# The first inverse's store on ScalarE's queue, a corner's copies ahead of a weight piece, and a chunk's keys behind three pieces

## The chip, the cores and the metric

One Trainium2 chip, one core of it. The metric is device time in microseconds (us), the median of several runs. The trace comes from one further execution under the hardware profiler; its times are counted from the start of its span. PE is TensorE, DVE VectorE, ACT ScalarE, POOL GpSimd, and SP is SyncE, which here only issues transfers.

## The reference: a delta-rule recurrence, then a multiplicative feed-forward

```python
# q, k, v: (4, 8, 768, 48) = batch, heads, steps, head size; beta: (4, 8, 768)
k_n = k / (np.linalg.norm(k, axis=-1, keepdims=True) + 1e-06)
for t in range(S):
    y[:, :, t] = np.einsum('bhd,bhde->bhe', q[:, :, t], state)
    v_old = np.einsum('bhde,bhd->bhe', state, kt)
    state = state + bt[:, :, :, None] * np.einsum('bhd,bhe->bhde', kt, vt - v_old)
x = y.transpose(0, 2, 1, 3).reshape(3072, 384)
out = ((x @ w1) * (x @ w2)) @ w3 @ w_out      # w1, w2: 384x1024; w3: 1024x1024; w_out: 1024x384
```

All of it is float32.

## The kernel before

**Chunks.** The 768 steps are cut into 12 chunks of 64. Inside a chunk the recurrence is a triangular solve. For each chunk `m`, `scores` (L357) multiplies keys by keys and by queries, and leaves `U` (L379, the scaled strictly triangular part) and `PT` (the masked products of keys and queries). The inverse of the unit triangular matrix is made in two steps. The diagonal 32x32 blocks of two chunks at a time are rearranged through DRAM: `to_blocks` stores them to `Ud` (L414, four transfers a chunk), `inverse(j)` loads them as `Ub` (L426), runs 31 elimination steps on DVE (L440 and L445), and stores the result to `Vd` (L453). For pairs 0 and 1 the elimination works in a PSUM bank, and ACT copies the result back to `Vb` (L449). Then `corner(m)` reads the blocks back: four transfers `TT<-Vd` (L462) and four `T22<-Vd` (L469). It makes the off-diagonal 32x32 corner with one DVE transpose (L481), two sets of products on PE (L498), and two ACT copies after each set (L514 and L525; the second writes the corner into `TT`).

**The chain over chunks.** `chain(c)` multiplies state and keys (L551, `S,KQ`), subtracts from the values (DVE, `R`, L584), multiplies by the inverse (L551, `R,TT`), scales (`X`, L594), multiplies by the keys and adds to the state (`S`, L613 or L615). `outputs(c)` makes y on PE (L652); ACT copies it to `xT` (L673), and transfers move some of its rows within SBUF (L684), six each for chunks 0 and 1.

**The feed-forward.** `w3 @ w_out` is folded into one matrix first (`transpose_w3`, L750 and L753, and `fold`, L759 and L766). Then `ab` multiplies `xT` by `w1` and `w2` (L779), ACT and DVE multiply the two (L791, L795), and later products with the folded matrix follow (L874). Weights come in 36 pieces: `piece` loads one into one of five `raw` buffers (L699), and ACT (L707, L708), DVE (L710, L711) and POOL (L715) rewrite it; after POOL's step the buffer is free. Pieces P24 to P29 are `w1`, P30 to P35 `w2`. `w2s` is at first the room of `w_out`, so P30 and its like also wait for folds.

**Queries and keys.** `load_perm(m)` loads a chunk's keys and then its queries in a permuted order, eight transfers each (L230: `kperm`, `qperm`), and DVE transposes them (L324). `p4.0` below is the keys of chunk 4, the fifth chunk.

**The order.** The order on every engine is fixed by hand. The text `ORDER` names generators: each word runs one more step of that part, and `in_text_order` (L159) ties the instructions of each engine to that order. So a word that stands later than another issues its instructions behind the other's on each engine that both use; on an engine that they don't share, nothing is ordered between them. Each engine, SP's queue too, works its line off in order and stands still at an instruction whose inputs or buffers are not ready. Steps that matter here, counted from 0:

- `P30.0` issues a piece's loads on SP, `P30.1` its ACT part, `.2` DVE, `.3` POOL.
- `V0.36` is the second of ACT's copies L449, `V0.37` the store of `Vd`; `V1.1` the load of `Ub`.
- `e0.0` is corner 0's eight copies on SP, `e0.1` DVE's L481, `e0.5` ACT's L525.
- `u2`, `u3` are the stores to `Ud`; `p4.0` the keys of chunk 4; `c1.0` to `c1.3` are chunk 1's `S,KQ`, `R`, `R,TT` and `X`.

SP issues every transfer, but for those of chunk 0's keys and queries at the start, which ACT issues.

Of the kernel before, what the change touches and what calls it, by code (L numbers as in the profile page):

```python
# [44 lines left out]
V0 P4 V0 P19 P19 P19 P6 f0 P16 P17 P17 V0 V0 P16 V0 V0 P17 P7 f2 k3 P14 p2 V0 V0 v1 P19 P15 f1  # L45
f0 g1 f1 t11 V0 d2 t11 P15 f2 f5 V0 P14 P15 f0 P16 v0 P17 V0 V0 V0 V0 g1 P20 f5 V0 f2 f5 t6 t9
P15 t6 P20 t7 V0 n1 P22 P20 V0 t7 d2 s0 V0 V0 f3 P23 P20 P22 t8 P21 V0 n0 P24 n0 f3 V0 V0 n1 t8
V0 V0 t9 V0 V0 s2 p3 f4 f3 P23 P22 P26 g1 V0 g1 V0 f4 g1 P21 P22 P23 t14 d3 f4 P23 g1 t12 p3 V0
N1 P30 t12 t14 t15 e0 t15 d3 f7 d3 f6 e0 P30 P21 e0 e0 P24 f7 s2 s2 e1 e0 s2 P24 e0 e1 V1 p4 s2
e1 P26 s2 e1 P25 d3 c0 P21 P30 u2 s3 c0 s3 P26 N1 P31 P24 y0 s3 s3 y0 c0 s3 s3 P25 t13 N1 e1 u3  # L50
P31 c0 P26 P31 P32 c1 V1 c1 e1 P25 V1 P27 c1 V1 c1 V1 V1 t13 V1 V1 V1 V1 V1 V1 y0 V1 P25 f7 f6
f6 P30 P32 P32 v2 V1 P27 s1 P31 V1 V1 y1 b3 b1 V1 b0 P32 P28 y1 b1 V1 b1 b3 P29 P27 b2 b3 y1 V1
P27 b1 b0 P29 P29 c1 a01 b2 a03 P28 V1 a01 a00 b3 P28 P29 a02 a02 a03 P35 P28 V1 a05 b7 a00 V1
V1 V1 V1 a06 P33 V1 b5 a05 b7 b0 V1 P34 V1 b5 V1 a06 V1 V1 V1 P34 k4 V1 P35 V1 g2 a00 V1 k5 a00
# [35 lines left out]
def kernel(  # L90
# [36 lines left out]
    def half(z):  # L127
        return slice(C * z, C * z + C)

    def feat(z):  # L130
        return slice(C * z, C * z + D)
# [6 lines left out]
    def in_turn(pool, shape, tag, n, name, dt=FP32):  # L138

        i = turns.get(tag, -1)  # L140
        while True:
            i = turns[tag] = (i + 1) % n
            if (tag, i) not in held:
                return pool.tile(shape, dt, tag=f"{tag}{i}", name=name, bufs=1)

    def two_banks():
        return in_turn(psW, [P, 2, 512], "w", 2, "ps_w")
# [11 lines left out]
    def in_text_order():  # L159
# [7 lines left out]
    pe, dve, act, pool, sync = nc.tensor, nc.vector, nc.scalar, nc.gpsimd, nc.sync  # L167
# [7 lines left out]
        out=strict[:], in_=strict[:], pattern=[[1, P]], compare_op=ALU.is_gt,  # L175
# [7 lines left out]
    def padded(name, shape, n, start=0):  # L183
        res = []
        for i in range(n):
            t = persist.tile(shape, FP32, name=f"{name}{i}")
            pool.memset(t[:, start:] if start else t[:], 0.0)
            res.append(t)
        return res

    TTs = padded("TT", [P, NR, H, C], 2)
# [3 lines left out]
    ktoks, vtoks, KQs, PTs, Xs, Ss = {}, {}, {}, {}, {}, {}  # L195
# [114 lines left out]
    def scale_of(x, m, crossed=0):  # L310
        j, cc = divmod(m, 2)
        return x[j][:, cc] if x is ns else x[j][:, crossed, cc]
# [92 lines left out]
    Uds, Vds = {}, {}  # L405
# [14 lines left out]
    def inverse(j):  # L420
        Vb = in_turn(work, [P, BS, BS], "Vb", 1, "Vb")
        pool.memset(Vb[:], 0.0)
        pool.memset(Vb[:].rearrange("p s t -> p (s t)")[:, 0 : BS * BS : BS + 1], 1.0)
        yield
        U = in_turn(work, [P, BS, BS], "Ub", 1, "Ub")
        sync.dma_start(out=U[:], in_=Uds.pop(j)[:])  # L426
        yield
        V = Vb
        if j < 2:

            V = two_banks().rearrange("p a (s t) -> p (a s) t", t=BS)
            held.add(("w", turns["w"]))
            for i in range(0, BS, BS // 2):
                act.copy(out=V[:, i : i + BS // 2], in_=Vb[:, i : i + BS // 2])
                yield
        for s in range(BS - 1):
            n = BS - 1 - s
            t = in_turn(work, [P, 256], "tb", 2, "tb")
            tv = t[:, 0 : (s + 1) * n].rearrange("p (r t) -> p r t", t=n)
            dve.tensor_tensor(  # L440
                out=tv, in0=V[:, 0 : s + 1, s : s + 1].to_broadcast([P, s + 1, n]),
                in1=U[:, s, s + 1 : BS].unsqueeze(1).to_broadcast([P, s + 1, n]), op=ALU.mult,
            )
            o = V[:, 0 : s + 1, s + 1 : BS]
            dve.tensor_tensor(out=o, in0=o, in1=tv, op=ALU.subtract)  # L445
            yield
        if j < 2:
            for i in range(0, BS, BS // 2):
                act.copy(out=Vb[:, i : i + BS // 2], in_=V[:, i : i + BS // 2])  # L449
                yield  # L450
            held.clear()
        Vds[j] = in_turn(dram, [P, BS, BS], "Vd", 2, "Vd")
        sync.dma_start(out=Vds[j][:], in_=Vb[:])  # L453
        yield

    T11s = padded("T11", [P, NR * H * BS + 8], 1, NR * H * BS)
# [75 lines left out]
    xts = {}  # L532

    def scaled_v(c):
        nv = vtoks[c]
        for r in range(NR):
            pool.tensor_tensor(  # L537
                out=nv[:, r], in0=nv[:, r],
                in1=scale_of(ns, c)[:, r].unsqueeze(2).to_broadcast([P, H, D]), op=ALU.mult,
            )  # L540
            yield

    def chain(c):
        TT, nv, KQ = TTs[c % 2], vtoks[c], KQs[c]

        def products(out, lhs, rhs):
            ps = two_banks()
            for r in range(NR):
                for h in range(H):
                    for z in range(2):  # L550
                        pe.matmul(  # L551
                            out(ps, r, h, z), lhsT=lhs(r, h, z), rhs=rhs(r, h, z),
                            start=True, stop=True,
                        )
            return ps[:, :, 0:DM].rearrange("p b (g d) -> p b g d", d=D)


        def crossed(ps, r, h, z):
            g = NP * r + h // 2
            return ps[half((z + h) % 2), h % 2, D * g : D * g + D]  # L560

        def by_tokens_of_features(ps, r, h, z):
            g = NP * r + h // 2
            return ps[half(z), h % 2, D * g : D * g + D]

        def by_features(ps, r, h, z):
            g = NP * r + h // 2
            return ps[feat(h % 2), z, D * g : D * g + D]

        def state(r, h, z):  # L570
            return St[feat(h % 2), z, NP * r + h // 2, :]

        St = Ss.get(c)
        R = nv
        if c > 0:
            ps = products(
                by_tokens_of_features, lambda r, h, z: KQ[feat(h % 2), NR * z + r, h // 2, 0, :], state
            )
            yield
            R = in_turn(work, [P, NR, H, D], "R", 1, "R")  # L580
            v3, r3 = (
                x[:].rearrange("p r (a e) d -> p (r a) e d", e=2) for x in (nv, R)
            )
            dve.tensor_tensor(  # L584
                out=r3, in0=v3, in1=ps.rearrange("p e g d -> p g e d"), op=ALU.subtract
            )
            yield
        ps = products(
            crossed, lambda r, h, z: TT[half(z), r, h, :], lambda r, h, z: R[half(z), r, h, :]
        )  # L590
        yield
        Xs[c] = X = in_turn(work, [P, NR, H, D], "X", 2, "X")
        for e in range(2):
            dve.tensor_tensor(  # L594
                out=X[:].rearrange("p r (a e) d -> p e (r a) d", e=2)[:, e], in0=ps[:, e],
                in1=scale_of(ws, c, 1).rearrange("p r (a e) -> p e (r a)", e=2)[:, e]
                .unsqueeze(2).to_broadcast([P, H, D]),
                op=ALU.mult,
            )
        yield  # L600
        if c < NCH - 1:
            kt = ktoks[c]
            ps = products(
                by_features,
                lambda r, h, z: kt[half((z + h) % 2), r, h, :],
                lambda r, h, z: X[half((z + h) % 2), r, h, :],
            )
            yield
            Ss[c + 1] = Sn = in_turn(work, [P, 2, H, D], "S", 2, "S")
            for z in range(2):  # L610
                f = feat(z)
                if c == 0:
                    dve.tensor_copy(out=Sn[f], in_=ps[f])  # L613
                else:
                    dve.tensor_tensor(out=Sn[f], in0=St[f], in1=ps[f], op=ALU.add)  # L615
            yield
# [348 lines left out]
    for m in range(NCH):  # L965
        parts[f"k{m}"] = lambda m=m: load_k(m, act.dma_start if m == 0 else sync.dma_start)
        parts[f"v{m}"] = lambda m=m: load_v(m)
        parts[f"p{m}"] = lambda m=m: load_perm(m)
        parts[f"d{m}"] = lambda m=m: by_vector(m)
        parts[f"s{m}"] = lambda m=m: scores(m)  # L970
        parts[f"u{m}"] = lambda m=m: to_blocks(m)
        parts[f"e{m}"] = lambda m=m: corner(m)
        parts[f"n{m}"] = lambda m=m: scaled_v(m)
        parts[f"c{m}"] = lambda m=m: chain(m)
        parts[f"y{m}"] = lambda m=m: outputs(m)
# [69 lines left out]
```

## Time and profile before

| | |
|---|---|
| three runs | 594.45, 594.7, 598.17 us; median 594.7 |
| the profiled execution | 593.18 us |
| its span, first to last instruction | 591.5 us |
| mean granted PE clock | 0.976 |
| PE, weight loads, DVE, ACT, POOL busy | 92%, 64%, 61%, 27%, 30% of the span |
| bytes over the span | 57.31 MB, mean 97 GB/s, in 219507 packets, 206656 of them under 512 bytes |

The busy share of the DMA, of PE and the PE clock change much along the span. In 40 equal slices of 14.8 us (tenths):

```profile
PE   2569898778999999999999989999999999999997
DVE  3897898569986579574796545865746924110012
PEclk9988999679999999999999999999999999999999
DMA  9989986668856455563553345614432040010001
```

The first six slices, to 89 us, have the DMA nearly full. In the next four, to 148 us, DMA and PE both have room, and the PE clock is at its lowest. From then on PE is full to the end. A duration or a wait in the first 150 us only counts if the work of the later slices starts later by it.

### The profile page before, as it was taken

How to read it: one execution, taken by the hardware profiler on the slowest of the kernel's cores; microseconds unless marked ns; L12 is line 12 of the kernel's file. 1: busy time of each engine (PE TensorE's matmuls, PEld its weight loads, DVE VectorE, ACT ScalarE, POOL GpSimd, SP SyncE). 2: the span in 40 equal slices, each digit the busy share in tenths (PEclk: the TensorE clock that was granted, in tenths of full speed). 3: DMA queues.
4: the chain of work that ended last, by engine and by line, in shares of the span. 5: the costliest groups of instructions: out<-in, count | busy, mean ns of one | idle time of the engine just before them, and what ended most of it. 6: DMA issues, size and time to landing. Idle time of an engine off the chain costs nothing.

```text
span 591.5 us, 19063 instructions
## 1 busy us (share of the span) xinstructions
PE 542.2 (92%) x8188; PEld 379.8 (64%) x8188; DVE 363.0 (61%) x828; ACT 159.3 (27%) x333; POOL 176.3 (30%) x223
## 2 busy tenths in 40 slices
PE   2569898778999999999999989999999999999997
PEld 2466555657878874558854669645698446974477
DVE  3897898569986579574796545865746924110012
ACT  4666354363412202121210232112121112311100
POOL 7563542033464601207121034111170000600051
PEclk9988999679999999999999999999999999999999
DMA  9989986668856455563553345614432040010001
GB/s 245 196 174 267 199 172 130 120 154 169 140 86 98 98 86 111 78 96 54 124 92 79 46 70 103 127 53 66 59 65 90 13 90 4 17 41 13 1 0 53
DMA packets 219507, 57.31 MB, mean 97 GB/s; under 512 B 206656, under 2 KB 212800, under 8 KB 219424
## 3 DMA queue, kind: packets, MB, share of 16 engines
q1 hardware_dynamic: 215232, 55.31, 46.9%
q10 hardware_dynamic: 4192, 0.79, 1.0%
q8 instruction: 64, 1.05, 0.8%
q14 instruction: 19, 0.16, 0.1%
HBM read 43.88 MB, written 11.01 MB: 93 GB/s over the span
## 4 chain that ended last, share of the span: by engine, by line
PE 70%; SPq 10%; DMA 9%; DVE 5%; issue 2%; ACT 1%; POOL 1%; DVEq 0%; POOLq 0%; ACTq 0%
PE ps_f L779 38%; PE ps_f L874 19%; DMA raw<-in_moe_w_dram 5%; PE ps_w L551 5%; PE ps_w L652 4%; SPq L230 3%; SPq L699 2%; PE ps_w L498 2%; DMA ktok<-in_k_dram 2%; DVE tb L440 1%; SPq L202 1%; DVE ps_w L445 1%; PE ps_w L367 1%; DMA Ub<-Ud 1%; PE ps_w L373 1%
## 5 line engine op out<-in xcount | busy, mean ns | idle before, releaser
L779 PE MATMUL ps_f<-xT,w2s 128*128 128x512 f32 (+1 forms) x336 | 131.8, 538 | 2.1 <-issue 2.1
L779 PE MATMUL ps_f<-xT,w1s 128*128 128x512 f32 (+1 forms) x336 | 128.0, 532 | 2.0 <-DMA xT<-xT 2.0
L846 POOL TENSOR_TENSOR ab<-ab 128x256 f32<-128x256 f32 x96 | 67.0, 727 | 175.3 <-DVE ab L795 153.6
L779 PEld LDWEIGHTS ps_f<-xT,w1s 128*128 128x128 f32 x336 | 63.3, 190 | 57.6 <-issue 52.2
L779 PEld LDWEIGHTS ps_f<-xT,w2s 128*128 128x128 f32 x336 | 62.0, 190 | 55.1 <-issue 51.9
L791 ACT COPY ab<-ps_f 128x512 f32<-128x512 f32 (+1 forms) x56 | 28.2, 526 | 165.8 <-PE ps_f L779 161.7
L874 PE MATMUL ps_f<-w,ab 128*128 128x192 f32 x376 | 66.3, 330 | 0.0
L874 PEld LDWEIGHTS ps_f<-w,ab 128*128 128x128 f32 x376 | 61.2, 190 | 4.2 <-issue 3.3
L795 DVE TENSOR_TENSOR ab<-ab,ps_f 128x512 f32<-128x512 f32 (+1 forms) x56 | 33.1, 603 | 48.9 <-PE ps_f L779 48.7
L440 DVE TENSOR_TENSOR tb<-Vb,Ub 128x31 f32<-128x31 f32 (+15 forms) x124 | 44.7, 360 | 17.2 <-DMA Ub<-Ud 13.9
L874 PE MATMUL ps_f<-room,ab 128*128 128x192 f32 x272 | 48.0, 330 | 0.8 <-DVE room L905 0.8
L445 DVE TENSOR_TENSOR Vb<-Vb,tb 128x31 f32<-128x31 f32 (+15 forms) x124 | 46.0, 371 | 4.3
L759 PE MATMUL ps_f<-w2s,w3T 128*128 128x384 f32 x128 | 45.5, 511 | 0.0
L874 PEld LDWEIGHTS ps_f<-room,ab 128*128 128x128 f32 x272 | 44.1, 190 | 1.6 <-issue 1.1
L673 ACT COPY xT<-ps_w 48x256 f32<-48x256 f32 x96 | 30.5, 366 | 54.4 <-PE ps_w L652 53.9
L270 POOL TENSOR_TENSOR sq<-ktok 128x384 f32<-128x384 f32 x24 | 20.7, 866 | 70.0 <-DMA ktok<-in_k_dram 39.5
L759 PEld LDWEIGHTS ps_f<-w2s,w3T 128*128 128x128 f32 x128 | 25.1, 202 | 16.5 <-issue 2.3
L537 POOL TENSOR_TENSOR vtok<-vtok,n 128x384 f32<-128x384 f32 x24 | 20.3, 859 | 43.1 <-DMA vtok<-in_v_dram 43.1
L367 PE MATMUL ps_w<-KQ 48*64 48x128 f32 x384 | 29.3, 293 | 1.7 <-DVE PT L397 1.7
L373 PE MATMUL ps_w<-KQ 48*64 48x64 f32 x768 | 30.1, 232 | 0.0
L715 POOL TENSOR_TENSOR w<-w,raw 128x512 uint32<-128x512 uint32 x16 | 20.6, 1294 | 29.0 <-issue 7.3
L373 PEld LDWEIGHTS ps_w<-KQ 48*64 48x64 f32 x768 | 27.2, 146 | 0.1
(109 smaller groups left out, 661.0 us busy)
## 6 DMA issues: line engine op xcount, KB each, us to landing
raw<-in_moe_w_dram SPq DMA_DIRECT2D x16, 512.0 KB, 6.5
vtok<-in_v_dram SPq DMA_DIRECT2D x24, 192.0 KB, 4.5
raw<-in_moe_w_dram SPq DMA_DIRECT2D x24, 192.0 KB, 4.7
out_dram<-osb SPq DMA_DIRECT2D x46, 96.0 KB, 2.0
ktok<-in_k_dram SPq DMA_DIRECT2D x44, 96.0 KB, 3.6
raw<-in_moe_w_out_dram SPq DMA_DIRECT2D x8, 384.0 KB, 4.4
Ud<-U SPq DMA_DIRECT2D x48, 64.0 KB, 2.6
Ub<-Ud SPq DMA_DIRECT2D x6, 512.0 KB, 4.1
```

The costliest lines, as they stand in the source:

```text
L367: pe.matmul(ps[half(z), 0, n : n + 128], lhsT=x[:, 0, :], rhs=x.rearrange("p j t -> p (j t)"), start=True, stop=True,)
L373: pe.matmul(ps[half(z ^ j), 1, n + C * j : n + C * j + C], lhsT=x[:, 0, :], rhs=x[:, j, :], start=True, stop=True,)
L440: dve.tensor_tensor(out=tv, in0=V[:, 0 : s + 1, s : s + 1].to_broadcast([P, s + 1, n]), in1=U[:, s, s + 1 : BS].unsqueeze(1).to_broadcast( ...
L445: dve.tensor_tensor(out=o, in0=o, in1=tv, op=ALU.subtract)
L551: pe.matmul(out(ps, r, h, z), lhsT=lhs(r, h, z), rhs=rhs(r, h, z), start=True, stop=True,)
L673: act.copy(out=xT[f, p:NP:2, b : b + NR, cc, :].rearrange("p a r t -> p r a t"), in_=pyv[f, z, b : b + NR],)
L759: pe.matmul(ps[:, 0:DM], lhsT=w3Ts[jc, kc // 4][:, kc % 4 * P : kc % 4 * P + P], rhs=wo[:, kc], start=(kc == 0), stop=(kc == KF - 1),)
L779: pe.matmul(ps[:].rearrange("p b c t -> p b (c t)"), lhsT=w[:, m, js], rhs=x[:, m, :, c0:c1].rearrange("p b c t -> p b (c t)"), start=(m = ...
L791: act.copy(out=t, in_=ps)
L795: dve.tensor_tensor(out=t, in0=t, in1=ps, op=ALU.mult)
L846: pool.tensor_tensor(out=o_, in0=x_, in1=y_, op=op)
L874: pe.matmul(ps[b][:, b, :], lhsT=abs_[u, HF * f + i][:, t0 : t0 + P], rhs=ws_[w][:, i], start=first and i == 0 and (b == 0 or n == "F"), s ...
```

## The change

Of the first inverse (`j == 0`) the store of `Vd` is issued by ACT instead of SP:

```diff
         Vds[j] = in_turn(dram, [P, BS, BS], "Vd", 2, "Vd")
-        sync.dma_start(out=Vds[j][:], in_=Vb[:])
+        (act if j == 0 else sync).dma_start(out=Vds[j][:], in_=Vb[:])
         yield
```

The values' tile is looked up where it is used, in `scaled_v` and in `chain`; this issues no other instruction:

```diff
     def scaled_v(c):
-        nv = vtoks[c]
         for r in range(NR):
             pool.tensor_tensor(
-                out=nv[:, r], in0=nv[:, r],
+                out=vtoks[c][:, r], in0=vtoks[c][:, r],
...
-        TT, nv, KQ = TTs[c % 2], vtoks[c], KQs[c]
+        TT, KQ = TTs[c % 2], KQs[c]
...
-        R = nv
+        R = vtoks.get(c)
...
-                x[:].rearrange("p r (a e) d -> p (r a) e d", e=2) for x in (nv, R)
+                x[:].rearrange("p r (a e) d -> p (r a) e d", e=2) for x in (vtoks[c], R)
```

And four lines of `ORDER` differ:

```diff
-V0 V0 t9 V0 V0 s2 p3 f4 f3 P23 P22 P26 g1 V0 g1 V0 f4 g1 P21 P22 P23 t14 d3 f4 P23 g1 t12 p3 V0
-N1 P30 t12 t14 t15 e0 t15 d3 f7 d3 f6 e0 P30 P21 e0 e0 P24 f7 s2 s2 e1 e0 s2 P24 e0 e1 V1 p4 s2
-e1 P26 s2 e1 P25 d3 c0 P21 P30 u2 s3 c0 s3 P26 N1 P31 P24 y0 s3 s3 y0 c0 s3 s3 P25 t13 N1 e1 u3
-P31 c0 P26 P31 P32 c1 V1 c1 e1 P25 V1 P27 c1 V1 c1 V1 V1 t13 V1 V1 V1 V1 V1 V1 y0 V1 P25 f7 f6
+V0 V0 t9 V0 V0 s2 p3 f4 f3 P23 P22 P26 g1 V0 g1 V0 V0 f4 g1 P21 P22 P23 t14 d3 f4 P23 g1 t12 p3
+N1 t12 t14 t15 e0 P30 t15 d3 f7 d3 f6 e0 P21 e0 e0 P24 P30 f7 s2 s2 e1 e0 s2 P24 e0 e1 V1 s2 e1
+P26 s2 e1 P25 d3 c0 P21 P30 u2 s3 c0 s3 P26 N1 P31 P24 y0 s3 s3 y0 c0 s3 s3 P25 t13 N1 e1 e1 u3
+c0 P26 P32 p4 c1 V1 c1 P25 V1 P27 c1 V1 P31 c1 P31 V1 V1 t13 V1 V1 V1 V1 V1 V1 y0 V1 P25 f7 f6
```

Engine by engine this comes to:

- SP, before: `Vd` store, P30, corner 0's copies, corner 1's copies, keys of chunk 4, P25, u2, P31, u3, P32, `Ub`. After: corner 0's copies, P30, corner 1's copies, P25, u2, P31, u3, P32, keys of chunk 4, `Ub`.
- ACT: the `Vd` store follows the two copies L449, ahead of P21. Before, P30's part stood ahead of corner 0's L514, with P24's behind it; after, both stand behind L514, P24's first, and still ahead of L525. Corner 1's L525 and the two copies L434 of the second inverse stand ahead of P31's part; before they stood behind it.
- DVE: P31's two instructions go from ahead of `R` of chunk 1 to behind its `X`.
- PE and POOL keep their order.

## The prediction

> **What bounds the kernel now.** I read the page first: PE is busy 92% of the span, and the chain of waits gives PE 70% and SP's queue 10%. Then PE's own waits, from 142 us to the end (columns: who waits on whom, us in total, times, longest).
>
> ```profile
> PE 70%; SPq 10%; DMA 9%; DVE 5%; issue 2%; ACT 1%; POOL 1%; DVEq 0%; POOLq 0%; ACTq 0%
> ...
> PE ps_f L779 <- issue: 2.1, 1, 2.1
> PE ps_f L779 <- DMA xT<-xT: 1.6, 1, 1.6
> PE ps_w L498 <- DVE T L481: 0.9, 1, 0.9
> PE ps_w L367 <- DVE PT L397: 0.9, 1, 0.9
> PE ps_f L874 <- DVE room L905: 0.8, 1, 0.8
> ```
>
> From 142 us PE is full: the rest is a fixed list of work, moved only by when it starts. The edit touches 84 to 127 us, where PE has holes. So I read the timelines of SP's queue, then ACT and PE, there (start, us, engine, line, operation, xcount, idle before and releaser).
>
> ```profile
> 83.82 4.33 SPq L230 DMA_DIRECT2D qperm<-in_q_dram  x8
> 88.24 0.43 SPq L453 DMA_DIRECT2D Vd<-Vb  x1
> 88.78 2.11 SPq L699 DMA_DIRECT2D raw<-in_moe_w_dram  x4
> 91.52 1.91 SPq L462 DMA_DIRECT2D TT<-Vd  x4
> ...
> 101.59 6.32 SPq L230 DMA_DIRECT2D kperm<-in_k_dram  x8
> 108.00 1.82 SPq L699 DMA_DIRECT2D raw<-in_moe_w_dram  x4
> 109.92 3.71 SPq L414 DMA_DIRECT2D Ud<-U  x4
> 113.73 3.17 SPq L699 DMA_DIRECT2D raw<-in_moe_w_dram  x4
> 117.00 2.01 SPq L414 DMA_DIRECT2D Ud<-U  x4
> 119.11 1.83 SPq L699 DMA_DIRECT2D raw<-in_moe_w_dram  x4
> 121.11 0.34 SPq L426 DMA_DIRECT2D Ub<-Ud  x1
> ```
>
> ```profile
> 84.00 1.07 ACT L449 COPY Vb<-ps_w 128x512 f32<-128x512 f32 x2 [2.68 <-DVE ps_w L445]
> ...
> 119.48 0.66 ACT L707 ACTIVATE w2s<-raw 128x512 f32<-128x512 f32 x1 [4.27 <-DMA raw<-in_moe_w_dram]
> 120.04 0.67 ACT L708 ACTIVATE raw<-raw 128x512 uint32<-128x512 uint32 x1
> 120.73 1.20 ACT L525 ACTIVATE TT<-ps_w 32x512 f32<-32x512 f32 x2
> ```
>
> ```profile
> 118.18 0.45 PE L551 MATMUL ps_w<-S,KQ 48*64 48x48 f32 x5 [0.75 <-issue]
> 122.41 2.08 PE L551 MATMUL ps_w<-R,TT 64*64 64x48 f32 x64 [3.78 <-ACT TT L525]
> ...
> 141.59 10.60 PE L779 MATMUL ps_f<-xT,w1s 128*128 128x256 f32 x48 [1.63 <-DMA xT<-xT]
> ```
>
> The reader is to see three things. SP issues almost without a pause. Vd's data was ready at 85.07 (L449's end) but its store waited in SP's line until 88.24. And PE lost 3.78 us at 118.63 because ACT held corner 1's last copies (L525; their matmuls ended at 115.72) behind piece P31, which waited for its DMA. PE's last late start of this stretch, 141.59, is again a transfer of SP's queue.
>
> [...] Nothing before shows a Vd store from ACT; SP's took 0.43 us to issue and 3.2 us to land, with the DMA 88% busy at 85 to 90 us. [...] TT<-Vd starts at 91.52, 0.1 us after Vd lands, and everything behind it stands. [...] PE was busy 1.66 us of 106 to 110, and the granted clock is 0.50 from 110 to 126.
>
> **The change, part by part.** The same instructions run; Vd's store of the first inverse alone changes queue, and the Python edits to vtoks issue nothing.
>
> *Store on ACT.* ACT issues it at about 85.1. An ACT issue of a load took 0.63 to 0.91 us; it is hidden, because ACT idles 1.17 us at 86.6 before L753, and P21, next on ACT, is not used by DVE until 96.32. Without that cover it would be 0.6 us on f3's copy. Landing: 3.2 us as on SP gives 88.3; the bounds are 2.6 (the least row of L453) and 6.7 (the slowest ACT load early on), so 87.7 to 91.8. I take 88.6. SP loses 0.53 of issue and the 0.63 us for which it waited for the landing.
>
> *Copies of corner 0 before P30.* SP comes to them at 88.24 with no filler in front: if Vd lands late, P30, corner 1 and all behind wait. From 88.6: eight copies 4.44 (91.52 to 95.96) to 93.0; P30 2.2 to 95.2; corner 1's eight 5.5 to 100.7. DVE's L481 for corner 0 can't follow by 3 us: its queue is full with the norms and L324 until 94.6, and L481 began at 95.69. So corner 0 gains 1.1 us, and PE with it. P30, issued from 93.1, lands 4.9 us later (as 88.78 did) at about 98.0, not 93.7. ACT now takes P24 first, and P30 stands there ahead of corner 0's L525, which is due at 99.6 (100.72 less 1.1): two ACT steps of 0.6 end at 99.2, so it just fits; each us of a later landing would come out of the gain. DVE used P30 only at 103.53.
>
> *Keys behind three pieces.* p4's eight DMAs (6.32 us) leave 101.6 and go behind P25, u2, P31, u3 and P32, directly ahead of Ub (L426). P25 1.9 to 102.6; u2 3.7 to 106.3 (its U was ready at 102.4, now 101.3); P31 3.2 to 109.5. Then u3 needs chunk 3's second U, ready at 112.45 before, so about 111.35: SP **idles** 1.9 us, or up to 4.9 if the stalls inside u2 and P31 (1.75 and 1.35 us over the normal issue) left with the keys. u3 2.0 to 113.4; P32 1.9 to 115.3; then the keys: 4.2 (eight of 0.53), 6.3 (as before) or 8.25 (the batch at 73.55). I take 5.2, since SP's pause lets the DMA drain: Ub at **120.5**, against 121.11. The ends are 119.5 and 123.6. The keys' readers (DVE from 166.67) have time.
>
> *Corner 1's copies before P31 on ACT, P31 after X on DVE.* L525 follows its matmuls at once, at about 114.7. R comes when S,KQ ends (118.63 less 1.1), so R,TT starts near 118.6 and PE reaches the first ab product (130.40) some 3.8 us sooner. **This is not kept:** that product reads xT's rows moved by L684, at 123.43 on SP behind Ub and P27; the last of them released PE at 131.96. PE waits there instead. P31 on DVE moves from 120.17 to about 122, before Ub lands at 127.2, so nothing. POOL keeps its order.
>
> *Sum.* What decides is SP: Ub, P27, xT, vtok, P28, P29, xT again (PE's start at 141.59), the loads, Vd at 158.52, TT, L481 at 165.20 and PE at 166.05. All follow SP's line. V1 (28.4 us of DVE from 127.29, without a gap) follows Ub, and its pieces follow SP. So the gain is that of Ub's issue: **0.6 us**. The profiled execution took 593.18 (span 591.5 and 1.68 around it), which makes 592.6; the median of the three runs is 1.5 above, so 594.1.
>
> Two costs not shown by the trace of before. PE's new idle time, some 126.4 to 131, can halve its clock again for the next products: 18 matmuls L779 are 4.2 us at full clock, so up to 4.2 more, less the 1.63 of waiting that they hide; 0 to 2.6, and I take 0. [...] And Ub may land in 4.1 us (the median) and not 6.1, which lets V1 start 2 us sooner, but its pieces still wait for SP: 0 to 1.5 gained; I take 0. The forecast's own range is 592.2 to 596.7.
>
> **The rivals.** *The PE hole is what counts:* the whole 3.78 us is kept, 590.9. For it: it is the longest PE wait after 90 us. Against: the releases by xT at 131.96 and 141.59. It would need SP to run 3 us ahead, so no stall of SP among the keys and u3's U some 2 us earlier. *The store gains nothing:* Vd lands near 91.5[...] SP stands from 88.2 with P30 behind it, and what is saved is spent: 594.7 to 596. *Slower: the keys push Ub back.* The keys are 8 x 32 x 16 = 4096 rows of 128 bytes or less, just ahead of Ub. With U of chunk 3 no earlier (112.5), u3 2.0, P32 with a stall 3.2, keys 8.25, Ub goes at 126.0, 4.9 us late, and V1, xT and the rest with it: 599.6. It decides from the point where the keys end after 121.1. For it: SP's wait at u3 is new, and the keys no longer fill it. Against: before u3 the DMA drains.
>
> **Chances.** Forecast 0.58, PE hole kept 0.08, store gains nothing 0.12, keys push Ub back 0.22. What a measurement of this kernel can tell from no change is about 1%, 5.9 us: under 588.8 lies none of the cases, over 600.6 only the last with more on top (a half clock). So faster 0.02, same 0.93, slower 0.05. The range, with the run at 598.17 among the three, is 591.6 to 598.8.
>
> **What would show it.** Right: Vd on ACT's queue near 85, TT<-Vd from 88.3 to 89, L481 near 94.6, no ACT wait before the second L525, R,TT on PE near 118.6, a pause of SP before the second Ud, Ub at 119.5 to 121.5, PE waiting 3 us or more for xT near 127 to 131, PE's x48 block near 141. Wrong: Ub after 123 (slower), no wait for xT and the x48 block before 138.5 (faster), or L481 still at 95.7.

## The result, and the profile after

The changed kernel is slower: 599.38 us in the median of 8 runs, against 594.58 of the kernel before beside it, a ratio of 1.008 with a 95% interval of 1.0054 to 1.0107. Its profiled execution took 599.53 us, with a span of 597.8.

The chain of waits of the changed kernel, the line of shares by engine: PE has grown to 76%, and SP's queue has shrunk to 6%. That doesn't say that SP matters less. Followed from the end, the chain now stays on PE down to the wait for `xT` that ends at 135.62; before, it left PE at 166.05 already.

```profile
PE 76%; DMA 9%; SPq 6%; DVE 4%; issue 2%; ACT 1%; POOL 0%; ACTq 0%; DVEq 0%; POOLq 0%
```

The timeline of SP's queue of the changed kernel (start, us, engine, line, operation, xcount; lines from 536 on have moved up by one):

```profile
81.73 7.24 SPq L698 DMA_DIRECT2D raw<-in_moe_w_dram  x4
89.06 4.08 SPq L230 DMA_DIRECT2D qperm<-in_q_dram  x8
93.19 2.08 SPq L462 DMA_DIRECT2D TT<-Vd  x4
...
106.36 3.27 SPq L414 DMA_DIRECT2D Ud<-U  x4
109.73 3.54 SPq L698 DMA_DIRECT2D raw<-in_moe_w_dram  x4
116.98 1.96 SPq L414 DMA_DIRECT2D Ud<-U  x4
119.03 2.74 SPq L698 DMA_DIRECT2D raw<-in_moe_w_dram  x4
121.82 4.86 SPq L230 DMA_DIRECT2D kperm<-in_k_dram  x8
126.73 0.49 SPq L426 DMA_DIRECT2D Ub<-Ud  x1
```

P26's four loads took 1.82 us before:

```profile
81.90 1.82 SPq L699 DMA_DIRECT2D raw<-in_moe_w_dram  x4
```

They take 7.24 now, so the q rows start at 89.06 and not 83.82. And `Ub` goes at 126.73 and not 121.11, with the pause before the second `Ud` (113.27 to 116.98) and the keys right in front of it. PE of the changed kernel:

```profile
122.98 2.06 PE L550 MATMUL ps_w<-R,TT 64*64 64x48 f32 x64 [1.10 <-DMA raw<-in_moe_w_dram]
...
135.62 6.40 PE L778 MATMUL ps_f<-xT,w1s 128*128 128x256 f32 x18 [4.75 <-DMA xT<-xT]
...
146.70 10.63 PE L778 MATMUL ps_f<-xT,w1s 128*128 128x256 f32 x48
```

The hole in front of `R,TT` is down from 3.78 us to 1.10, as meant. But the wait for `xT` is 4.75 us, and the x48 block, from which PE is full, starts 5.1 us later (141.59 before). That is about the measured 4.8 us.

What P26 waited for is in the critical chain of the changed kernel around 85 us (start, us, what):

```profile
83.60 1.08 ACT Vb L449 x2
84.68 0.02 issue
84.70 2.63 DMA Vd<-Vb
87.34 0.02 issue
87.35 0.32 SPq L698
87.72 0.78 SPq L698
88.54 0.42 SPq L698
```

P26's first load went at 81.73, and its second at 87.35, 0.02 us after the store from ACT had landed (84.70 and 2.63). No data passes from one to the other. What ties the load to the store is left open here; experiments 1 and 3 ask whether the two are tied, and not merely late at one time.

So two things stand as suspects: P26's wait for the landing of the store from ACT, and the keys in front of `Ub`, which the prediction had as its slower rival. The expectations below name the first the counter theory, the second the keys theory, and both together the two-part theory, in which nothing else of the change costs. The first name stands for the wait alone.

### The profile page after: what moved, and what is told of

The parts are those of the page before. It is cut to its first block, busy times and chain, and to the rows that moved or that the text cites. A ratio compares the mean times of both kernels' runs of the same rounds, so it can differ in the third digit from the quotient of the medians.

```text
span 597.8 us, 19061 instructions
## 1 busy us (share of the span) xinstructions
PE 544.2 (91%) x8188; PEld 381.0 (64%) x8188; DVE 368.2 (62%) x828; ACT 159.8 (27%) x333; POOL 176.2 (29%) x223
## 4 chain that ended last, share of the span: by engine, by line
PE 76%; DMA 9%; SPq 6%; DVE 4%; issue 2%; ACT 1%; POOL 0%; ACTq 0%; DVEq 0%; POOLq 0%
PE ps_f L778 43%; PE ps_f L873 17%; PE ps_w L550 5%; PE ps_w L651 4%; DMA raw<-in_moe_w_dram 3%; PE ps_w L498 2%; PE ps_w L367 2%; DMA Ub<-Ud 2%; SPq L230 2%; PE ps_w L373 1%; SPq L414 1%; DMA ktok<-in_k_dram 1%; DMA X<-in_q_dram 1%; DVE tb L440 1%; SPq L202 1%
## 5 line engine op out<-in xcount | busy, mean ns | idle before, releaser
L778 PE MATMUL ps_f<-xT,w1s 128*128 128x512 f32 (+1 forms) x336 | 130.0, 540 | 4.8 <-DMA xT<-xT 4.8
L778 PEld LDWEIGHTS ps_f<-xT,w1s 128*128 128x128 f32 x336 | 65.0, 195 | 60.6 <-issue 51.9
L514 ACT COPY T<-ps_w 32x512 f32<-32x512 f32 x24 | 13.8, 575 | 52.8 <-PE ps_w L498 52.5
```

Of the source, the lines that this page charges most:

```text
L778: pe.matmul(ps[:].rearrange("p b c t -> p b (c t)"), lhsT=w[:, m, js], rhs=x[:, m, :, c0:c1].rearrange("p b c t -> p b (c t)"), start=(m = ...
```

## The experiments

Every experiment is compared with the kernel before on the same chip, over 8 runs or more; ratios are to that kernel, with 95% intervals. The profiled execution of a kernel is one of its runs, and not always a typical one: in run 2 it was the fastest of 22 (590.24 us), in run 7 it lay over 2 us above the median (597.45). Run N is the one of section N below. Lines of `ORDER` are cut at the right where nothing differs.

### 1. The store ordered behind P26's loads

The store keeps its queue and its place on ACT. It is only tied, without a wait, to come behind P26's last load in the order of the program.

```diff
+    last_piece = []
...
+            last_piece.append(sync.dma_start(   # in piece()
...
-        (act if j == 0 else sync).dma_start(out=Vds[j][:], in_=Vb[:])
+        st = (act if j == 0 else sync).dma_start(out=Vds[j][:], in_=Vb[:])
+        if j == 0:
+            in_order(last_piece[-1], st.ins)
```

> The changed kernel[...]. Counter theory (SP stood 5.3 us at the second load of P26[...]): P26's four loads take about 1.8 us, the q rows start near 83.7 and not 89.06, the copies of corner 0 near 88.5, Ub is issued at 119.5 to 122; 593 to 595.5 us. Keys theory (the keys ahead of Ub are what costs): Ub stays near 126, 598.5 to 600.

Ratio 1.0032 (1.0008 to 1.0055), against 1.008 of the changed kernel. SP's timeline of this kernel (its lines have moved down by up to three):

```profile
80.73 1.82 SPq L701 DMA_DIRECT2D raw<-in_moe_w_dram  x4
82.66 5.37 SPq L231 DMA_DIRECT2D qperm<-in_q_dram  x8
88.07 2.08 SPq L465 DMA_DIRECT2D TT<-Vd  x4
...
104.26 1.98 SPq L701 DMA_DIRECT2D raw<-in_moe_w_dram  x4
113.04 1.97 SPq L415 DMA_DIRECT2D Ud<-U  x4
115.11 2.92 SPq L701 DMA_DIRECT2D raw<-in_moe_w_dram  x4
118.07 5.07 SPq L231 DMA_DIRECT2D kperm<-in_k_dram  x8
123.19 0.49 SPq L427 DMA_DIRECT2D Ub<-Ud  x1
```

With the same bytes, queue and place, P26 is back at 1.82 us: the 5.3 us for which it stood hung on the order of the store and P26's loads in the program, and not on the load of the DMA, which was 0.88 busy here from 80 to 90 and 0.46 in the changed kernel. The other half of the keys theory also shows: SP stands from 106.24 to 113.04 in front of the second `Ud`, the keys then take 5.07 us, and `Ub` goes 2.1 us later than before. Neither theory's number was met; both hold in part.

### 2. The store back on SP, the order of the change kept

```diff
-        (act if j == 0 else sync).dma_start(out=Vds[j][:], in_=Vb[:])
+        sync.dma_start(out=Vds[j][:], in_=Vb[:])
```

> The changed kernel with the first store back on SP, right behind P26's loads; the order is otherwise that of the change. Counter theory: no wait at P26, SP waits about 1 us for the store's data and goes on near 85; corner 0's copies near 89.5, 594 to 596 us. Keys theory: Ub after 124, 598.5 to 600.

Ratio 1.0028 (1.0006 to 1.0049), median 594.0. P26 took 1.82 us, SP then waited for the store's data and sent it at 85.67, and `Ub` went at 121.70. So the new order, with the keys in it, costs about 0.3%, with or without the new queue.

### 3. Only the queue: the store on ACT in the kernel before

```diff
-        sync.dma_start(out=Vds[j][:], in_=Vb[:])
+        (act if j == 0 else sync).dma_start(out=Vds[j][:], in_=Vb[:])
```

> The kernel before, with the first store on ACT's queue and nothing else. The store[...] stands later on ACT (behind a copy of the fold, near 86.6). Counter theory: SP stands at P26 from about 82.7 until the store lands near 89, some 6 us, and the kernel is slower by 3 to 6 us: 597.5 to 600.5. Keys theory: the keys are where they were, so no loss: 593.5 to 595.

Ratio 1.0073 (1.0046 to 1.0099). Here it is P26's third load that waits. The chain shows it, with a later time of the store:

```profile
86.24 2.63 DMA Vd<-Vb
88.89 0.31 SPq L699
89.24 0.42 SPq L699
```

The third load goes at 88.89, 0.02 us after the store lands. The wait is on another load than in the changed kernel, and it ends later as the store does: both times 0.02 us after the landing (87.33 and 88.87). The keys are at their old place, and `Ub` still goes at 125.28: this one word is enough for nearly the whole loss.

### 4. Only the keys, in the kernel before

```diff
-P31 c0 P26 P31 P32 c1 V1 c1 e1 P25 V1 P27 c1
+P31 c0 P26 P31 P32 p4 c1 V1 c1 e1 P25 V1 P27 c1     # and p4 taken out of the line with "V1 p4 s2"
```

> The kernel before, with the keys of chunk 4 behind P25, P31 and P32 and nothing else. Keys theory: Ub goes at 124 or later, 598 to 600. Counter theory: SP waits a little for the second U and the keys then take 4 to 6 us; Ub at 121 to 123, 594.5 to 596.5.

Ratio 1.0029 (1.0007 to 1.005). SP's timeline of this kernel:

```profile
106.61 3.36 SPq L699 DMA_DIRECT2D raw<-in_moe_w_dram  x4
113.06 1.96 SPq L414 DMA_DIRECT2D Ud<-U  x4
115.12 2.94 SPq L699 DMA_DIRECT2D raw<-in_moe_w_dram  x4
118.11 4.62 SPq L230 DMA_DIRECT2D kperm<-in_k_dram  x8
122.78 0.49 SPq L426 DMA_DIRECT2D Ub<-Ud  x1
```

The keys used to fill the time in which chunk 3's second U is not yet made. Taken away, they leave SP standing for 3.1 us (109.97 to 113.06), and then take 4.62 us on top. `Ub` goes 1.7 us late.

### 5. The keys back, P26's wait left

```diff
-c0 P26 P32 p4 c1 V1      # in the changed kernel; p4 stands again behind "e1 V1"
+c0 P26 P32 c1 V1
```

> The changed kernel with the keys of chunk 4 back at their old place[...]. Two-part theory: SP still stands some 5 us at the second load of P26 until the store lands near 87.3; the keys then fill the pause before the second Ud, which still waits for its U until 116 to 117, so Ub goes at 121 to 123 and not 126.7: 595 to 597 us (ratio 1.002 to 1.006), so the two costs are not a plain sum. Rival (keys alone are the cause): as before, ratio 0.998 to 1.001.

Ratio 1.0045 (1.002 to 1.0069). P26 takes 7.66 us, its second load goes at 88.54 as the store lands (85.89 and 2.63), and `Ub` at 123.89, a little later than expected. The rival's range is missed.

### 6. Neither: the store ordered behind P26's loads and the keys back

The edits of experiments 1 and 5 together.

> The changed kernel without either suspect: the store on ACT[...], and the keys of chunk 4 back between corner 1's copies and P25. Two-part theory[...]: corner 0's copies at 88 to 88.5, no pause of SP at the second Ud, Ub at 119 to 121; 0 to 1.5 us faster than before, ratio 0.9975 to 1.0. Rival (the order of corner and pieces costs too): slower than before by 1 us or more, ratio 1.002 or above.

Ratio 1.0006 (0.9985 to 1.0028). Corner 0's copies start at 88.44, and `Ub` goes at 119.88. The loss is gone. A gain isn't there either: the expected end of 0.9975 lies below the interval, and a gain of up to 0.15% can't be told from none.

The four corners of the square are then, by ratio: both 1.008, P26's wait alone 1.0045 (run 5), keys alone 1.0032 (run 1), neither 1.0006. They were measured on more than one chip, each against the kernel before on its own. The two costs, 0.45% and 0.32%, add up to 0.77% of the 0.80%; the intervals are too wide to tell a plain sum from a small overlap.

### 7. The keys further back, behind the first moves of xT

The edit of experiment 1, and `p4` behind `y0` in the line that ends in `f7 f6`.

> [...] the keys of chunk 4 further back still, behind Ub, P27 and the six moves of xT for chunk 0. If the keys cost because they stand ahead of Ub, V1 and the first xT: Ub near 118, first ab product near 127, 592.5 to 594 (ratio at most 1.0). If they cost because SP stood idle earlier and the sum of issues up to the second xT is what counts: the moves of xT for chunk 1 stay near 136.5, PE waits there instead, ratio 1.001 to 1.004.

Ratio 1.0031 (1.0012 to 1.005), the second case. `Ub` went at 120.24, before its old time, and nothing was won by it:

```profile
129.39 5.81 PE L781 MATMUL ps_f<-xT,w1s 128*128 128x256 f32 x18 [1.81 <-DMA xT<-xT]
...
144.92 13.06 PE L781 MATMUL ps_f<-xT,w1s 128*128 128x256 f32 x48 [4.98 <-DMA xT<-xT]
```

PE starts the first products sooner and then waits 4.98 us for the second set of moves, which SP issued from 140.25. (The moves were expected near 136.5; U of chunk 3 was late too, with the second `Ud` at 115.20 after a pause of SP from 110.08. The x48 block also ran 13.06 us and not 10.60, at a granted clock of 0.50 from 144 to 149.) The ratio is that of run 1, so it isn't their place before `Ub` that makes the keys dear. SP's idle time in front of the second `Ud` fits both places that were tried.

### 8. Only corner 1's copies and P31, in the kernel before

```diff
-P25 t13 N1 e1 u3 / P31 c0 P26 P31 P32 c1 V1 c1 e1 P25 V1 P27 c1 V1 c1 V1
+P25 t13 N1 e1 e1 u3 / c0 P26 P32 c1 V1 c1 P25 V1 P27 c1 V1 P31 c1 P31 V1
```

> The kernel before with one part of the change: corner 1's last copies ahead of P31 on ACT, and P31 behind X of chunk 1 on DVE; SP's queue is untouched. Prediction's view: PE's wait of 3.8 us for L525 at 118.6 goes, and PE waits for xT instead, its x48 block stays at 141 to 142; ratio 0.998 to 1.001. Rival (the PE hole counts): 3 to 4 us faster, ratio 0.993 to 0.995.

Ratio 1.0008 (0.9986 to 1.003). PE of this kernel:

```profile
119.07 2.07 PE L551 MATMUL ps_w<-R,TT 64*64 64x48 f32 x64 [1.11 <-issue]
129.45 4.47 PE L779 MATMUL ps_f<-xT,w1s 128*128 128x256 f32 x18 [1.35 <-DMA xT<-xT]
...
141.44 10.99 PE L779 MATMUL ps_f<-xT,w1s 128*128 128x256 f32 x48 [1.52 <-DMA xT<-xT]
```

The 3.78 us in front of `R,TT` are down to 1.11 (it starts at 119.07 and not 122.41), and the x48 block starts at 141.44 as before (141.59). This PE wait, which is followed by one for SP's line, was worth nothing that the interval shows. The rival that the hole counts is out.

### 9. A version meant to beat both

The kernel of experiment 6, with the six moves of `xT` for chunk 0 on ACT, behind their copies and tied, without a wait, to come behind P31's loads in the order of the program.

```diff
-                    sync.dma_start(
+                    mv = (act if c == 0 else sync).dma_start(
...
+                    if c == 0:
+                        in_order(last_piece[-1], mv.ins)
-P24 y0 s3 s3 y0 c0     # ORDER: y0's last step comes up
+P24 y0 s3 s3 y0 y0 c0
```

> A version meant to beat both: store on ACT and xT's six moves of chunk 0 on ACT right behind their copies[...]; keys at their old place, corner order of the change. If SP's line up to the second xT sets when PE becomes full: SP has six issues less, xT of chunk 1 at 131 to 134, PE's x48 block 1 to 3 us earlier, ratio 0.995 to 0.999. Rival (the second inverse, from Ub's landing on, is the next to be late, and PE waits at its L498 near 166 instead): ratio 0.999 to 1.002.

Ratio 0.9981 (0.996 to 1.0001). PE no longer waited for `xT`. SP came to the second `xT` at 133.29, inside what was expected, but late in it, since its pieces took 7.31 us in front of it; and the six issues held ACT from 113.57 to 118.47, so that corner 1's last copies (L525 before) ran at 119.76. The middle of the interval is a gain of 1.1 us, and the interval just reaches no change, so it isn't shown that this version is faster.

## Why the prediction was wrong

The range (591.6 to 598.8) missed the measured 599.4, and the sign was the other one.

- **The store on ACT is where it failed.** The sum charged the store with its issue on ACT and its landing, and named as waiting for it only corner 0's copies. It said that SP "loses 0.53 of issue and the 0.63 us for which it waited for the landing". What runs 1 and 3 showed in its place is that a transfer of SP which needs nothing from the store waits for it: 5.3 us at P26, worth 0.45 to 0.73% of the time by runs 1, 3 and 5. The wait had no row in the trace of before, and no bound was set for it. The landing itself was no trouble: at 87.33 it came a little before the earliest bound (87.7), 2.63 us after an issue at 84.70. So the rival in which the store lands near 91.5 is out too.
- **"A pause of SP before the second Ud" was right in kind, and "the keys 5.2" in size.** The keys took 4.6 to 5.1 us once they stood behind it. As forecast, the DMA had less to do in the pause: it was 0.41 busy from 110 to 120 in run 1, and 0.74 before. But the pause, put at 1.9 us and 4.9 at most, was 3.1 in run 4, 3.7 in the changed kernel and 6.8 in run 1. Two other terms of that sum were short: U of chunk 3, due at 111.35, let the second `Ud` go at 113.04 and 113.06 only, and P32 took 2.9 and not 1.9 us. So `Ub` went at 122.8 to 123.2 and not 120.5 (runs 1 and 4), and the keys cost 0.3% where 0.6 us of gain were forecast for the whole.
- **The gain on corner 0 was half there.** The copies start at 88.07 in run 1 as foreseen (88.6), and L481 2.0 us earlier than before (93.71 and 95.69). But chunk 3's U came no earlier for it (112.32 to start in run 1, 111.76 before); the last section has where PE lost the lead. Run 6 has everything but the two costs, and shows no gain beyond its interval.
- **The slower rival had the time and half the reason.** Its 599.6 us and `Ub` at 126.0 came out almost as said (126.73). But it got there by the keys alone, with every term at its upper end; alone, the keys gave `Ub` at 122.8 to 123.2. Agreement in the total was no proof of the mechanism.
- **"This is not kept" was right.** PE's hole in front of `R,TT` was closed, and the time went into the wait for `xT` (run 8, and 4.75 us in the changed kernel). One reading in front of it was short: L525 ended at 121.93, but `R` on DVE, behind P31 there, at 122.31, and `R,TT` began at 122.41. The change moved both.
- **The half clock came, and its term was put at 0.** After 4.75 us of idling PE's 18 products took 6.40 us, and 4.47 in run 8 after 1.35 us of waiting; the granted clock was 0.50 from 134 to 140, and 1.00 in run 8 from 129 to 134. This is 1.9 us, inside the 0 to 2.6 given. It is part of the loss: the x48 block followed without a wait, though the move of `xT` that released it before had landed at 144.88, so by an estimate from these times some 1.7 us of its 5.1 are the clock's.
- **How long PE idles before the half clock is not settled.** In these runs idling was followed by the half clock, but not after one length: beside the 4.75 us of the changed kernel, the 18 products took 5.81 us after waits of 2.50 us in run 1 and of 1.81 in run 7, with a granted clock of 0.51 (133 to 136) and 0.50 (130 to 132). The prediction's own case was 1.66 us busy in 4, with 0.50 from 110 to 126.

The store from ACT landed no sooner than such stores had from SP: 2.63 us after its issue in the changed kernel and 3.39 in run 1, where SP's six of before took 2.6 to 3.2. ACT's queue was to save SP 0.53 us of issue; what it cost was 5.3 us at P26. The prediction had seen SP's line stand at a transfer that waits (`TT<-Vd`, until 91.52), and P26's second load, until 87.35, is one more such case, which the prediction did not count.

## What to carry to other kernels

After a transfer is moved to another queue, look in the trace for a transfer of the old queue that goes just as the moved one lands. Here one that needed nothing from the store stood 5.3 us and went 0.02 us after the landing; an order without a wait between the store and P26's loads took that wait from P26 (run 1). Work that fills a wait for data can be free where it stands; here it cost time at both places tried behind the wait. Look for the last wait of the full engine before it stays full: a hole ahead of that one is worth closing only if that one moves too.

## What the runs showed that was not expected

- SP's line is held by landings as well as by issue times. In run 1 the wait for the store falls on the last of the eight q rows: it goes at 87.72, 0.02 us after the store from ACT (84.31 and 3.39) has landed. Another stop stays open: in the changed kernel the third load of P31 took 2.14 us to issue from 110.67, and what held it is not shown.
- Between the two parts of chunk 0's product with `TT` (64 matmuls), PE stood for 0.27 us before, 1.64 after, 2.79 in run 1, 1.90 in run 6 and 0.19 in run 4, and the profile names no releaser. This is of the size of the gains sought here, and in runs 1 and 6 it took back corner 0's lead: in run 1 the first part ended at 101.98 (104.00 before), and the second began at 104.77 (104.26 before). The traces point to a possible cause, which no run tested. The pages list a DMA queue for instructions (packets, MB, share):

```profile
q8 instruction: 64, 1.05, 0.8%
```

Of the 36 pauses of PE over 0.15 us without a named releaser between 98 and 123 us in the eleven traces, 35 end 1.2 to 1.6 us after a packet of this queue has ended (before: 102.86 and 104.26; run 1: 103.23 and 104.77). So PE may have stood there for its next instructions; what these packets carry was not shown. In run 1 the packet ended no sooner than before.
